# Weights copied by transfer, the last products taken tile by tile, and a new written order

## The chip, the cores and the metric

The kernel runs on one core of one Trainium2 chip. The time is device microseconds of one execution, the median of several: 563.26 us before (three runs, 563.24 to 565.26). The engines are TensorE (PE, with its weight loads as PEld), VectorE (DVE), ScalarE (ACT), GpSimd (POOL) and SyncE (SP), which issues nearly all transfers from one queue.

## The reference, cut to what matters

```python
# attention: B=4 batches, H=8 heads, S=768 steps, D=48; MoE: 3072 tokens, 384 -> 2048 -> 384
scale = np.minimum(mag, 0.999) / (mag + 1e-06)            # mag = |a_re + i a_im|
for t in range(S):
    new_re = ar * S_re - ai * S_im                        # complex decay of the state
    new_im = ar * S_im + ai * S_re
    S_re, S_im = new_re + outer(k[t], v[t]), new_im
    y[t] = q[t] @ S_re
x = y.transpose(0, 2, 1, 3).reshape(B * S, H * D)
h = x @ w_in
out = (np.maximum(h, 0) + np.log1p(np.exp(-np.abs(h)))) @ w_out
```

## The kernel before, in words

The 768 steps are cut into six groups of 128 (g = 0 to 5). In each group four chunks, one a batch, go through the recurrence in its parallel form, and the 512 tokens that they give go through the two products.

`pre` (L328) loads the decays and q and k of one or two chunks and turns them, with logarithms, exponentials, sines and running sums on ACT and DVE, into scaled q and k. `chunk` (L533) sends them by transfer into another layout (L565, L569), forms scores on PE (L633 in group 0, L637 later), masks them on DVE into the tiles `a` (L642, L645), multiplies them with v and the earlier state (L674, L677), splits the result into two float32r words in `xt` (L686, L687) and updates the state (L712, L716). From group 1 on, all of this runs PE on tiles of 32 columns or rows; everything else uses the array whole.

`moe` (L730) runs, for each of 16 blocks f of 128 hidden columns, a first product of nine matmuls of 512 columns (`mm1`, L755), a softplus (ACT L759 to L761, DVE L770 or L764), a split into `gh` and `gl` (DVE L772 or ACT L773, DVE L774), and a second product of nine matmuls (`mm2`, L790) into three banks o0, o1, o2, one for each 128 rows of the output. In group 0 the second product takes the weights as they came, in three slower float32 matmuls (L787). After it, `move` (L289) makes the two-word form of the eight w_out blocks: a copy into a free buffer `t` (L291 on ACT or L293 on DVE), a rounding (L276 or L278) and a subtraction (L279). `fin` and `closing` copy the three banks out and send them (L814 to L816, L801 and L802). Weights come as 64-bit words; `inspect` (L303) reads them again for a check, whose count (`verdict`, L890) every engine loads at the end (L915, L1149) to branch past the general program.

The planner records every operation as a task with its readers and writers. The order in which tasks are issued, and for some of them the engine (A or D behind a number), stands in the table ORDER, written out by hand; entries x and y are filler matmuls that nothing reads (L828). Buffers come from pools by tag: `t` has five, `g` six (gh, gl, two of the v tiles), `lt` two (softplus), `a` two (masked scores), `att` three banks.

Of the kernel before, what the change touches and what calls it, by code (L numbers as in the profile page):

```python
# [21 lines left out]
P = 128  # L22
# [17 lines left out]
NLT = 2  # L40
NG = 6
# [3 lines left out]
LAG = 2  # L45
NTM = 1
# [117 lines left out]
class Prog:  # L164
# [64 lines left out]
    def weights(self):  # L229
# [5 lines left out]
        for j in range(2 * NWP):  # L235
# [92 lines left out]
    def pre(self, si):  # L328
# [163 lines left out]
        def turn():  # L492
            if summed:
                for c in range(m):
                    h = slice(c * W // m, (c + 1) * W // m)
                    ab, va, _ = sums(1, c, f"o{1 + si % 2}" if first else "att", 1 if first else NATT, (part(t3, c), v3))
                    add("DVE", d1(W // m), lambda h=h, va=va: V.tensor_scalar(vn()[:, h], va(), 1.0 / TWO_PI, None, ALU.mult),
                        r=[ab], w=[part(t5, c)])
# [7 lines left out]
            add("DVE", d2(W), lambda: V.tensor_scalar(vn(), v4(), 1.0 / TWO_PI, None, ALU.mult), r=[t4], w=[t5])  # L506
# [26 lines left out]
    def chunk(self, si, c):  # L533
# [43 lines left out]
        if not last and not turned:  # L577
            for j in range(2):
# [15 lines left out]
                add("PE", 0.25, trans, r=[q for q in rs if q[1] != (zc, 1 - j)], w=[pst])  # L594
# [3 lines left out]
        if not last and turned:  # L598
            for j in range(2):
                def blocks(j=j):  # L600
                    X = half().rearrange("p (j i k t) -> p j i k t", j=2, i=NI, k=2)[:, j, :, 1]
                    o = kt().rearrange("p (q b j i) -> p j i q b", q=NQ, b=QT, j=2)[:, j]
                    V.transpose(o, X.rearrange("p i (q b) -> p i q b", q=NQ))  # L603

                add("DVE", d1(DM), blocks, r=[q for q in rs if q[1] != (zc, 1 - j)], w=[(kt, j)])
# [85 lines left out]
        if not last:  # L691
# [27 lines left out]
            add("PE", 1.5 if first else 0.75, kvmm, r=[k2 if turned else kt, vt] + ([] if first else [vo]), w=[kv], mode=0 if first else 1)  # L719
# [10 lines left out]
    def moe(self, g, dst):  # L730
# [13 lines left out]
        def mm1(f):  # L744
            h = Buf(ps, "h", [P, 512], F32, "h", 2)
            t = Buf(p, "lt", [P, GT], F32, "lt", NLT)
# [11 lines left out]
            add("PE", 9 * tmm, mm, r=[xt, w], w=[h])  # L758
# [19 lines left out]
        def mm2(f):  # L778
            gt = gs.pop(f)
            w = self.w["o", f // 2]  # L780

            def mm():
                for m in range(NI):
# [9 lines left out]
            t = add("PE", 2.57 if native("o", f) else 9 * tmm, mm, r=[*gt, w], w=acc)  # L793
# [3 lines left out]
        def closing(m):  # L797
            o = Buf(p, "t", [P, NI * 2 * CH], F32, "o", NT)

            def leave():  # L800
                A.activation(o()[:, :n], acc[m](), AF.Copy)  # L801
                nc.scalar.dma_start(dst[m * P : (m + 1) * P], o()[:, :n].rearrange("p (b t) -> p b t", b=B))  # L802
# [3 lines left out]
        def fin():  # L806
            for m in range(NI):
                if g == NGRP - 1 and m == NI - 1:
# [21 lines left out]
    def fast(self):  # L830
        with ExitStack() as ctx:
# [44 lines left out]
            cols = self.out.rearrange("d (b s) -> d b s", b=B)  # L876
            for g in range(NGRP):
                self.moe(g, cols[:, :, g * CH : (g + 1) * CH])
# [117 lines left out]
    def tokens(self):  # L996
        tc, nc = self.tc, self.nc
        V, A, G, PE = nc.vector, nc.scalar, nc.gpsimd, nc.tensor
        with ExitStack() as ctx:
# [22 lines left out]
            flat = self.toks.rearrange("b s n -> (b s) n")  # L1022
            with tc.For_i(0, NTOK, P) as t0:
                x = p.tile([P, DM], F32, tag="x", name="x")
                nc.sync.dma_start(x, flat[bass.ds(t0, P)])
# [38 lines left out]
                nc.sync.dma_start(self.out.rearrange("(m p) t -> p m t", p=P)[:, :, bass.ds(t0, P)],  # L1064
# [4 lines left out]
5 0 4 3 24 8 9 43 2 1 27 28 10 11 12 13 62 14 30 29 31 15 46 47 32D 16 33 48 17 795 49 65 821 34 18 66 50 44 805 35  # L1069
51 67 68 63 6 796 69 36 52 25 19 22 822 70D 37 823 797 53 y1 x2 38 81 87 54 798 39 82 88 83 55 20 40 801 89 84 56 21  # L1070
91 85 86 42 71 y2 x4 57 92 45 7 26 41 815 103 102 23 93 125 72 73 126 y4 x1 133 58 64 94 127 74 128 59 106 96 61 107
75 104 144 131 y3 x3 76 114 90 97 145 100 98 77 78 99 80 130 132 134 806 115 129 x3 137 101 111 138 110 95 135 142
147 150 146 148 149 136 152 108 109 105 139 143 799 112 151 163 113 824 164 140A 153 800 802 156 154 161 155 157 171
816 141 172 162 803 817 118 169 170 158 818 119 159A 819 116 117 160 166 60 165 168 167 173 807 79 175 811 182 120
121A 123 188 174 176 845 825 820 808 122 177 178A 180 179 976 189 809 804 812 977 978 979 971 190 813 191 810 980
846 871 831 208 841 192 861 972 973 974 975 826 x3 987 847 827 848 981 193 865 184 183 835 855 988 989 194 990 991
814 828 195 982 983 203 984 849 196 986 992 204 993 985 850 829D 999 197 994 995 998 205 830 198 1000 206 851 199
996 214 1001 997 207A 215 1002 200 1004 201 1005 1003 216 1010 1011 1006 124 1016 1007 1008 217 832 218 833 834 202
836 1009 837 219 229 1012 1013 230 838 231 232 839 1014 842 1015 1029 1022 255 840 1030 233 238 1031 1032 181 220
1028 1017 240 1033 221 222 223 856 843 237 234 236 185 254 235 1023 844 857 1018 1019 256 242 1020 241 239 858 224  # L1080
1021 244 257 1035 245 243 225 249 268 859 186 251 252 253 209 258 1024 1025 261 246 1026 247A 187 1036 226 250 1027
262 1034 227 272 860 269 270 278 210 279 1037 1038 266 259 260 1041 263 228 271A 1039 281 280 282 852 853 854 1047
1040 1042 1043 1044 866 867 248 283 293 868 296 1048 869 1049 1046 1052 870 1045 1050 297 862 316 213 318 1051 863
864 294 872 267 315 317 212 1059 295 300 1053 319 1060 284 285 1054 264 1055 1061 1062 286 1056 287 1058 1064 1082D
265 323 1083 299 325 873 874 320 1073 1057 321 301 298 326 1063 288 322D 324 1065 1066 1074 289 308 1075 273 1084
290 327 309 306 291 328A 1069 1067 307 1070 330 310 329 331 292 304 311A 211 1068 1071 302 312 332 333 334 1097 336
1072 305 303 313 314 1098 1099 1100 1111 335 1101 1102 1104 342 343 1112 1103 1113 1114 345 344 1105 1106 1107 1115
346 347 1076D 1108 1109 1077D 1118 1119 1127 1110 357 1116 1078 1117 1126 360 358 1120 1121 1134 1128 1122 1129 1130
361 366 385 1079 359 368 1123 1143 348 337 382 367D 386D 1124 1125 383 274 380 1080 381 275 1131 365 379 1144 384
1145 1132 349 362 363 364 276 1146 1081 350 369 1133 1147 396 1142 1135 1148A 1136 1151 1149 377 389 387 1137 1138  # L1090
1139 351 397 352 353 1152 1140A 1153 1141 398 390 354 355 356 388 1150 1159 400 277 1158 1154 406 407 1155 401 394
391 408 409 1160 1156A 1161 395 1183 1162 370 410 392A 399 393 1085 372 371 1163 1166 373 1167 374 1086D 1157 411
421 422 424 423 412 1164A 1184 1165 413 378 1185 1186 1187 1188 1189 1168 375A 429 338 376 426 427 1169 1170 428 339
# [111 lines left out]
```

## Time and profile before

| what | us |
| --- | --- |
| median of 3 runs | 563.26 |
| the profiled execution, as timed | 563.96 |
| its span, first to last instruction | 562.3 |
| PE busy | 539.1 |
| DVE busy | 440.4 |
| ACT busy | 419.8 |

The page's slices show PE at nine tenths or more from the second slice of 14 us to the last but one, at the full clock. So what counts is when PE's unbroken work starts, how much work it is, what gaps are left, and what comes after its last matmul.

### The profile page before, as it was taken

How to read it: one execution, taken by the hardware profiler on the slowest of the kernel's cores; microseconds unless marked ns; L12 is line 12 of the kernel's file. 1: busy time of each engine (PE TensorE's matmuls, PEld its weight loads, DVE VectorE, ACT ScalarE, POOL GpSimd, SP SyncE). 2: the span in 40 equal slices, each digit the busy share in tenths (PEclk: the TensorE clock that was granted, in tenths of full speed). 3: DMA queues.
4: the chain of work that ended last, by engine and by line, in shares of the span. 5: the costliest groups of instructions: out<-in, count | busy, mean ns of one | idle time of the engine just before them, and what ended most of it. 6: DMA issues, size and time to landing. Idle time of an engine off the chain costs nothing.

```text
span 562.3 us, 13185 instructions
## 1 busy us (share of the span) xinstructions
PE 539.1 (96%) x5438; PEld 420.7 (75%) x5438; DVE 440.4 (78%) x693; ACT 419.8 (75%) x716; POOL 5.7 (1%) x27
## 2 busy tenths in 40 slices
PE   1999999999999999999999999999999999999995
PEld 1688656755788788877878888788888887888883
DVE  7999999999899999989888798978895434352342
ACT  7986998686598986677858659668777647758884
POOL 4000000000000000000000000000000000000000
PEclk9999999999999999999999999999999999999998
DMA  8679914507518062285453573552644722143532
GB/s 313 261 192 365 413 54 113 163 0 186 156 39 235 30 154 89 72 237 174 122 165 110 136 203 104 135 173 65 150 125 125 203 57 85 56 128 125 161 93 59
DMA packets 49584, 81.90 MB, mean 146 GB/s; under 512 B 4336, under 2 KB 33776, under 8 KB 49520
## 3 DMA queue, kind: packets, MB, share of 16 engines
q1 hardware_dynamic: 48992, 80.76, 48.1%
q8 instruction: 43, 0.70, 0.5%
q10 hardware_dynamic: 528, 0.26, 0.2%
q14 instruction: 21, 0.17, 0.1%
HBM read 54.26 MB, written 7.86 MB: 110 GB/s over the span
## 4 chain that ended last, share of the span: by engine, by line
PE 77%; DVE 11%; ACT 7%; issue 2%; DMA 2%; SPq 0%; DVEq 0%; ACTq 0%
PE h L755 30%; PE o L790 26%; PE o L787 6%; PE att L637 4%; PE att L674 2%; PE att L677 2%; DVE t L428 2%; DVE kt L603 1%; PE att L633 1%; PE att L716 1%; PE att L584 1%; ACT L887 1%; DVE a L645 1%; DMA x<-dense_dram 1%; DMA out_dram<-o 1%
## 5 line engine op out<-in xcount | busy, mean ns | idle before, releaser
L755 PE MATMUL h<-xt,wi 128*128 128x512 f32 x864 | 217.5, 400 | 1.7 <-DVE lt L770 1.0
L755 PEld LDWEIGHTS h<-xt,wi 128*128 128x128 f32 x864 | 160.3, 188 | 44.8 <-issue 3.4
L790 PE MATMUL o<-gh,wo 128*128 128x512 f32 x480 | 160.8, 398 | 0.0
L759 ACT ACTIVATE lt<-h 128x512 f32<-128x512 f32 x96 | 56.8, 593 | 72.5 <-PE h L755 51.0
L770 DVE SCALAR_TENSOR_TENSOR lt<-h,lt 128x512 f32<-128x512 f32 x80 | 54.7, 687 | 71.1 <-ACT lt L761 70.8
L790 PEld LDWEIGHTS o<-gh,wo 128*128 128x128 f32 x480 | 90.2, 188 | 21.9 <-issue 0.6
L790 PE MATMUL o<-gl,wo 128*128 128x512 f32 x240 | 94.6, 394 | 0.3 <-DVE gl L774 0.3
L761 ACT ACTIVATE lt<-lt,fixed 128x512 f32<-128x512 f32 x96 | 68.6, 720 | 2.0
L774 DVE TENSOR_TENSOR gl<-lt,gh 128x512 fp32r<-128x512 f32 x80 | 54.3, 687 | 12.5 <-ACT gh L773 7.5
L760 ACT ACTIVATE lt<-lt 128x512 f32<-128x512 f32 x96 | 60.0, 629 | 2.0
L790 PEld LDWEIGHTS o<-gl,wo 128*128 128x128 f32 x240 | 45.2, 188 | 10.6 <-DVE gl L774 0.9
L787 PE MATMUL o<-gf,raw_wo 128*128 128x512 f32 x96 | 43.2, 594 | 0.2 <-DVE raw_wo L269 0.2
L887 ACT ACT_TABLE_LOAD x30 | 38.5, 1283 | 0.5
L428 DVE TENSOR_TENSOR_SCAN t<-hold,t 128x384 f32<-128x384 uint8 x40 | 36.1, 945 | 0.8
L645 DVE TENSOR_TENSOR a<-att,mask 128x512 f32<-128x512 f32 x40 | 26.8, 685 | 8.4 <-PE att L677 4.7
L787 PEld LDWEIGHTS o<-gf,raw_wo 128*128 128x128 f32 x96 | 17.8, 190 | 19.5 <-issue 17.2
L637 PEld LDWEIGHTS att<-qk 96*32 96x32 f32 x1280 | 25.1, 110 | 5.9 <-issue 3.3
L773 ACT ACTIVATE gh<-lt 128x512 fp32r<-128x512 f32 x28 | 17.3, 626 | 14.7 <-DVE lt L770 13.9
L637 PE MATMUL att<-qk 96*32 96x64 f32 (+3 forms) x1280 | 27.8, 235 | 0.1
L772 DVE TENSOR_SCALAR gh<-lt 128x512 fp32r<-128x512 f32 x52 | 21.8, 424 | 6.1 <-PE o L790 4.3
L477 ACT ACTIVATE x<-t 128x768 f32<-128x768 f32 x20 | 16.2, 836 | 10.1 <-DVE t L428 10.1
L524 DVE TENSOR_TENSOR x<-x,t 128x768 f32<-128x768 f32 x24 | 22.7, 951 | 0.5
(110 smaller groups left out, 681.0 us busy)
## 6 DMA issues: line engine op xcount, KB each, us to landing
x<-dense_dram SPq DMA_DIRECT2D x20, 768.0 KB, 6.1
qk<-x SPq DMA_DIRECT2D x48, 288.0 KB, 4.3
raw_wi<-w_in_dram SPq DMA_DIRECT2D x8, 768.0 KB, 9.5
raw_wo<-w_out_dram SPq DMA_DIRECT2D x8, 768.0 KB, 11.7
seen<-w_in_dram SPq DMA_DIRECT2D x16, 384.0 KB, 3.5
seen<-w_out_dram SPq DMA_DIRECT2D x16, 384.0 KB, 3.6
v<-vpad_dram SPq DMA_DIRECT2D x24, 224.0 KB, 4.4
qk<-x SPq DMA_DIRECT2D x48, 96.0 KB, 3.6
```

The source lines that it names most:

```text
L428: V.tensor_tensor_scan(out()[:, s], self.hold, inc()[:, s], 0.0, ALU.mult, ALU.add)
L637: PE.matmul(psc()[QT * u : QT * (u + 1), hh * P + f : (hh + 1) * P], q[:, h, CH + f : CH + f + QT], q[:, h, f:CH], start=True, stop=True)
L645: V.tensor_tensor(a().rearrange("p (x z) t -> p x z t", z=2), psc().rearrange("p (x z t) -> p x z t", x=2, z=2), self.mask[:, None].to_bro ...
L755: PE.matmul(h()[:, :n], w()[:, q, i, fs], xt()[:, x, i], start=k == 0, stop=k == 3 * NI - 1)
L759: add("ACT", a1(n) - 0.04, lambda: A.activation(tv(), h(), AF.Abs), r=[h], w=[t])
L760: add("ACT", a1(n), lambda: A.activation(tv(), tv(), AF.Exp, scale=-1.0), w=[t], tab="log")
L761: add("ACT", a1(n, 1), lambda: A.activation(tv(), tv(), AF.Ln, bias=self.one), w=[t], tab="log")
L770: add("DVE", d1(n), lambda: V.scalar_tensor_tensor(tv(), h(), 0.0, tv(), ALU.max, ALU.add), r=[h], w=[t])
L774: add("DVE", d1(n), lambda: V.tensor_tensor(gl(), tv(), gh().bitcast(F32), ALU.subtract), r=[t, gh], w=[gl])
L787: PE.matmul(acc[m]()[:, :n], v, gt[0](), start=f == 0, stop=f == NF - 1)
L790: PE.matmul(acc[m]()[:, :n], w()[:, wq, f % 2, ms], x(), start=f == 0 and q == 0, stop=f == NF - 1 and q == 2)
L887: nc.scalar.preload_act_table_set(TABLES[table])
```

## The change

- The copy in `move` becomes a transfer from SyncE's queue, out of the raw weights into a buffer `t`; ACT and DVE keep the rounding and the subtraction.
- In the last group the second products of the last four blocks f are twelve tasks of three matmuls, one for each f and bank, so that the written order can finish o0, then o1, then o2. Three matmuls of one f and bank are done as before.
- The output in memory is laid out by group, so that a row of one output transfer is 512 floats in one run (2 KB) instead of four runs of 128 (512 B); the host puts it back in order. The general program, which isn't run here, follows.
- `a`, `lt` and `g` share one pool of ten buffers, where they had two, two and six.
- Two more operations may be given to ACT, and some planning durations differ.
- ORDER is another sequence throughout, with 23 filler matmuls instead of 26 (ten of 512 columns in both).

```diff
-NLT = 2
-NG = 6
+NG = 10
+LAST = 4
...
-                x = add("ACT", a1(n), lambda: A.activation(bits()[:, :n].bitcast(F32), val().bitcast(F32), AF.Copy),
-                        r=[raw], w=[bits])
-                x.alt["DVE"] = (d2(n), lambda: V.tensor_copy(bits()[:, :n].bitcast(F32), val().bitcast(F32)))
+                add("SP", 0.45, lambda: nc.sync.dma_start(bits()[:, :n], val()), r=[raw], w=[bits], nbytes=4 * n * P)
...
+                    q.alt["ACT"] = (a1(W // m) - 0.05, lambda h=h, va=va: A.activation(vn()[:, h], va(), AF.Copy, scale=1.0 / TWO_PI))
...
-            a = Buf(p, "a", [P, 4, P], F32, f"a{gc}_{j}", 2)
+            a = Buf(p, "g", [P, 4, P], F32, f"a{gc}_{j}", NG)
...
-            t = Buf(p, "lt", [P, GT], F32, "lt", NLT)
+            t = Buf(p, "g", [P, GT], F32, "lt", NG)
...
-        def mm2(f):
-            gt = gs.pop(f)
+        def mm2(f, part=range(NI)):
+            gt = gs[f]
...
-                for m in range(NI):
+                for m in part:
...
-                    dst[ms], ov().rearrange("p (b t) -> p b t", b=B)), r=[o], nbytes=4 * n * P)
+                    dst[ms], ov()), r=[o], nbytes=4 * n * P)
...
+        split = NF - LAST if g == NGRP - 1 else NF
         for f in range(NF + LAG):
             if f < NF:
                 mm1(f)
-            if f >= LAG:
+            if LAG <= f < split + LAG:
                 mm2(f - LAG)
+        for m in range(NI):
+            for f in range(split, NF):
+                mm2(f, (m,))
         fin()
...
-                self.moe(g, cols[:, :, g * CH : (g + 1) * CH])
+                self.moe(g, self.out[:, g * GT : (g + 1) * GT])
...
-1764 1768
+1767 1771 1772 1774 1768 1773 1775 1776
```

Three places in the program show what the new sequence does. The first is PE's end, in the last group; o0, o1 and o2 are the output banks, gh and gl the two words of one block f. Before, the last nine matmuls are the last block's:

```order
L790 MATMUL o0_5554<-gh_5967,wo7_2329 128x512
L790 MATMUL o0_5554<-gl_5979,wo7_2329 128x512
L790 MATMUL o0_5554<-gh_5967,wo7_2329 128x512
L790 MATMUL o1_5558<-gh_5967,wo7_2329 128x512
L790 MATMUL o1_5558<-gl_5979,wo7_2329 128x512
L790 MATMUL o1_5558<-gh_5967,wo7_2329 128x512
L790 MATMUL o2_5562<-gh_5967,wo7_2329 128x512
L790 MATMUL o2_5562<-gl_5979,wo7_2329 128x512
L790 MATMUL o2_5562<-gh_5967,wo7_2329 128x512
```

After, the last twelve are all of bank o2, from four blocks f:

```order
L790 MATMUL o2_5569<-gh_5903,wo6_2248 128x512
L790 MATMUL o2_5569<-gl_5905,wo6_2248 128x512
L790 MATMUL o2_5569<-gh_5903,wo6_2248 128x512
L790 MATMUL o2_5569<-gh_5892,wo6_2248 128x512
L790 MATMUL o2_5569<-gl_5920,wo6_2248 128x512
L790 MATMUL o2_5569<-gh_5892,wo6_2248 128x512
L790 MATMUL o2_5569<-gh_5923,wo7_2334 128x512
L790 MATMUL o2_5569<-gl_5942,wo7_2334 128x512
L790 MATMUL o2_5569<-gh_5923,wo7_2334 128x512
L790 MATMUL o2_5569<-gh_5956,wo7_2334 128x512
L790 MATMUL o2_5569<-gl_5958,wo7_2334 128x512
L790 MATMUL o2_5569<-gh_5956,wo7_2334 128x512
```

So o1 is complete twelve matmuls before the end instead of three, and o0 twenty-one instead of six.

The second place is PE in group 1, between the scores of two chunks (qk7 and qk6; att0 to att2 are the banks, x_5 the turned q and k, gf the softplus of a block of group 0). Before, a transpose and six second-product matmuls stand between them:

```order
L637 MATMUL att1_92<-qk7_1239 32x128
L584 MATMUL att0_91<-ident_58,x_5_623 128x128 x3
L787 MATMUL o0_193<-gf_1346,raw_wo7_619 128x512
L787 MATMUL o1_695<-gf_1346,raw_wo7_619 128x512
L787 MATMUL o2_697<-gf_1346,raw_wo7_619 128x512
L787 MATMUL o0_193<-gf_1355,raw_wo7_619 128x512
L787 MATMUL o1_695<-gf_1355,raw_wo7_619 128x512
L787 MATMUL o2_697<-gf_1355,raw_wo7_619 128x512
L637 MATMUL att1_92<-qk6_1267 32x128
```

After, the same two chunks' scores follow each other, as do later their products with v:

```order
L637 MATMUL att0_91<-qk7_1256 32x96
L637 MATMUL att0_91<-qk7_1256 32x64
L637 MATMUL att0_91<-qk7_1256 32x32 x2
L637 MATMUL att0_91<-qk7_1256 32x64
L637 MATMUL att0_91<-qk7_1256 32x96
L637 MATMUL att0_91<-qk7_1256 32x128
L637 MATMUL att2_93<-qk6_1277 32x128
L637 MATMUL att2_93<-qk6_1277 32x96
```

PE changes between the whole array and its 32-wide tiles 74 times in the program before and 62 times in the one after.

The third place is SyncE's queue in the same stretch (vo, v: parts of v; x_6, x_7: inputs of the next chunks; o: output copies). Before:

```order
L569 DMA qk6_1267<-x_5_623 96x1x256
L565 DMA qk6_1267<-x_5_623 96x1x768
L569 DMA qk6_1267<-x_5_623 96x1x256
L565 DMA qk6_1267<-x_5_623 96x1x768
L388 DMA x_6_1082<-dense_dram 128x2x768
```

After, two of the eight weight copies (valo0, valo3) stand among these transfers:

```order
L565 DMA qk7_1256<-x_5_510 96x1x768 x2
L291 DMA valo0_1275<-raw_wo0_254 128x768
L565 DMA qk6_1277<-x_5_510 96x1x768
L569 DMA qk7_1256<-x_5_510 96x1x256
L291 DMA valo3_1301<-raw_wo3_512 128x768
L569 DMA qk6_1277<-x_5_510 96x1x256 x2
```

The queue issues in order, so what stands behind a copy also stands behind the wait for the copy's buffer.

## Rows read from the trace of the kernel before

**Rows 1.** Busy time of each engine in four stretches: us, busy (instructions), PE clock, DMA share, GB/s

```profile
0.00:33.60 33.60, 20.67 (x104) 14.79 (x104) 28.91 (x58) 29.26 (x56) 5.71 (x27) 1.00 0.77 268
33.60:58.00 24.40, 24.30 (x295) 21.89 (x295) 23.84 (x38) 16.67 (x35) 0.00 (x0) 1.00 0.92 312
58.00:546.00 488.00, 484.78 (x4999) 376.82 (x5000) 383.21 (x587) 364.82 (x607) 0.00 (x0) 1.00 0.46 132
546.00:562.30 16.30, 9.35 (x42) 7.23 (x40) 4.42 (x12) 9.00 (x21) 0.00 (x0) 0.90 0.19 51
```

**Rows 2.** Busy tenths in 40 slices of 14 us, from the page

```profile
DVE  7999999999899999989888798978895434352342
```

**Rows 3.** Waits of PE over the span: us in total, times, longest

```profile
PE sum L449 <- DVE t L419: 12.2, 1, 12.2
PE h L755 <- DVE lt L770: 1.0, 1, 1.0
```

**Rows 4.** PE from its first scores to the second pair of first products

```profile
33.59 2.05 PE L633 MATMUL att<-qk 96*128 96x128 f32 x16
...
52.78 4.46 PE L755 MATMUL h<-xt,wi 128*128 128x512 f32 x18
...
58.41 4.46 PE L755 MATMUL h<-xt,wi 128*128 128x512 f32 x18 [0.51 <-DVE gf L764]
```

**Rows 5.** Chain of waits, 545 us to the end

```profile
546.90 8.35 PE o L790 x36
...
555.33 0.60 ACT o L801
```

**Rows 6.** The last output transfer, on ACT's queue

```profile
L802 ACTq DMA_DIRECT2D out_dram<-o x1: 647/647/647, 556.0 to 556.0; - x1
...
DMA to landing us min/median/max: 4.8/4.8/4.8
```

**Rows 7.** The closing branch by engine: ns min/median/max, first and last start

```profile
L1149 SPq EVENT_SEMAPHORE  x8: 17/17/17, 557.8 to 560.9; - x8
...
L1149 ACTq EVENT_SEMAPHORE  x1: 17/17/17, 558.2 to 558.2; - x1
```

**Rows 8.** The two output transfers on SyncE's queue at the end

```profile
L816 SPq DMA_DIRECT2D out_dram<-o x2: 534/540/547, 554.5 to 555.3; - x2
...
DMA to landing us min/median/max: 2.6/2.7/2.8
```

**Rows 9.** The last block's softplus and split, in order of time

```profile
547.81 0.58 ACT L759 ACTIVATE lt<-h 128x512 f32<-128x512 f32 x1
...
551.11 0.69 DVE L774 TENSOR_TENSOR gl<-lt,gh 128x512 fp32r<-128x512 f32 x1
```

**Rows 10.** What the transfers moved, in 40 slices: 557 to 560 us, then the span

```profile
GB/s 273 300 287 314 307 294 267 287 260 280 259 273 280 287 266 294 294 280 280 396 55 130 225 14 123 0 0 0 0 0 0 0 0 0 0 7 14 7 0 0
...
GB/s 313 261 192 365 413 54 113 163 0 186 156 39 235 30 154 89 72 237 174 122 165 110 136 203 104 135 173 65 150 125 125 203 57 85 56 128 125 161 93 59
```

**Rows 11.** Chain of waits, 325 to 346 us: start, us, what

```profile
325.11 1.24 PE att L637 x34
326.36 2.31 PE o L790 x9
328.67 2.10 PE h L755 x9
...
344.88 1.11 PE att L637 x34
```

**Rows 12.** The copies of w_out by engine: busy us, mean ns, idle before

```profile
L291 ACT ACTIVATE valo<-raw_wo 128x768 f32<-128x768 f32 x5 | 4.1, 835 | 0.0
...
L293 DVE COPY valo<-raw_wo 128x768 f32<-128x768 f32 x3 | 1.7, 552 | 0.0
```

**Rows 13.** Transfers of the same size: KB each, us to landing

```profile
kd<-kt SPq DMA_DIRECT2D x8, 384.0 KB, 3.9
```

**Rows 14.** Who waited for output transfers: us, times

```profile
  ACT kt L586: 1.9, 1
```

More of the change, by code (lines that the diff above doesn't have):

```diff
@@ L505, in turn @@
             add("DVE", st, lambda: scan(1, v4, v3), r=[car[1]], w=[t3, t4] + ([] if last else [car[1]]))
-            add("DVE", d2(W), lambda: V.tensor_scalar(vn(), v4(), 1.0 / TWO_PI, None, ALU.mult), r=[t4], w=[t5])
+            q = add("DVE", d2(W) + 0.04, lambda: V.tensor_scalar(vn(), v4(), 1.0 / TWO_PI, None, ALU.mult), r=[t4], w=[t5])
+            q.alt["ACT"] = (a1(W), lambda: A.activation(vn(), v4(), AF.Copy, scale=1.0 / TWO_PI))
             add("DVE", d1(W), lambda: V.scalar_tensor_tensor(v3(), v4(), 1.0 / TWO_PI, vn(), ALU.mult, ALU.subtract),
@@ L592, in evac @@
                     copy(common[:, :, :, :, j], p3[:, :, 2 * D :].rearrange("p i (y r) -> p i y r", y=2))
-                add("PE", 0.25, trans, r=[q for q in rs if q[1] != (zc, 1 - j)], w=[pst])
+                add("PE", 0.32, trans, r=[q for q in rs if q[1] != (zc, 1 - j)], w=[pst])
                 q = add("ACT", 0.43, evac, r=[pst], w=[(kt, j)])
@@ L603, in blocks @@
                     V.transpose(o, X.rearrange("p i (q b) -> p i q b", q=NQ))
-                add("DVE", d1(DM), blocks, r=[q for q in rs if q[1] != (zc, 1 - j)], w=[(kt, j)])
+                add("DVE", 0.74, blocks, r=[q for q in rs if q[1] != (zc, 1 - j)], w=[(kt, j)])
             spill = self.dram.tile([P, NI * 2 * CH], F32, tag=f"kd{gc}", name=f"kd{gc}")
@@ L717, in kvmm @@
                                   start=h == 0, stop=h == H - 1)
-            add("PE", 1.5 if first else 0.75, kvmm, r=[k2 if turned else kt, vt] + ([] if first else [vo]), w=[kv], mode=0 if first else 1)
+            add("PE", 1.33 if first else 0.6, kvmm, r=[k2 if turned else kt, vt] + ([] if first else [vo]), w=[kv], mode=0 if first else 1)
             def reals(t):
@@ L756, in mm @@
                         k += 1
[L758 removed]
+            add("PE", 9 * tmm + 0.012, mm, r=[xt, w], w=[h])
             add("ACT", a1(n) - 0.04, lambda: A.activation(tv(), h(), AF.Abs), r=[h], w=[t])
@@ L791, in mm @@
                                   start=f == 0 and q == 0, stop=f == NF - 1 and q == 2)
-            t = add("PE", 2.57 if native("o", f) else 9 * tmm, mm, r=[*gt, w], w=acc)
+            t = add("PE", (2.57 if native("o", f) else 9 * tmm) * len(part) / NI, mm, r=[*gt, w], w=[acc[m] for m in part])
             if self.opener is None:
@@ L1020, in convert @@
                 V.tensor_tensor(lo, v, hi.bitcast(F32), ALU.subtract)
-            flat = self.toks.rearrange("b s n -> (b s) n")
-            with tc.For_i(0, NTOK, P) as t0:
+            cols = self.out.rearrange("(m p) (g b t) -> p m g b t", p=P, g=NGRP, b=B)
+            rows = self.toks.rearrange("b (g t) n -> t g b n", t=CH)
+            with tc.For_i(0, NGRP, 1) as g, tc.For_i(0, B, 1) as b:
                 x = p.tile([P, DM], F32, tag="x", name="x")
-                nc.sync.dma_start(x, flat[bass.ds(t0, P)])
+                nc.sync.dma_start(x, rows[:, bass.ds(g, 1), bass.ds(b, 1)].rearrange("t g b n -> t (g b n)"))
                 px = ps.tile([P, 512], F32, tag="px", name="px")
@@ L1203 @@
     r = run_bass_kernel_spmd(nc, [{f"{n}_dram": arr[n] for n in _INS}], core_ids=[0])
-    return np.ascontiguousarray(r.results[0]["out_0_dram"].T)
+    out = r.results[0]["out_0_dram"].reshape(DM, NGRP, B, CH)
+    return np.ascontiguousarray(out.transpose(2, 1, 3, 0)).reshape(NTOK, DM)
```

139 lines of the change are left out of this document (72 added, 67 removed), and 6 rows, old and new, of the table ORDER.

## Prediction

> **What bounds the kernel now.** I read the busy times by stretch first, then PE's waits, then the chain of waits, then the end line by line. In the long stretch from 58 to 546 us PE is busy for 484.78 of 488.00 us [rows 1]: 3.2 us are idle. DVE has 105 us to spare there and ACT 123 us, though the page's slices show DVE at nine tenths or more in 15 of slices 2 to 17, which end at 239 us [rows 2]. Before 58 us PE waits once for long, 12.2 us at the start, for the first decay sums; its longest other wait is 1.0 us [rows 3]. From 33.59 us PE works on without a gap (24.30 of 24.40 us [rows 1]) through the scores of group 0 to its first products at 52.78 us [rows 4]. After 546.90 us come 36 matmuls, 8.35 us, which end at 555.25 us [rows 5], and then 7.0 us with next to no engine at work. So a time is to be won in four places: the start of unbroken work, the work itself, 3.2 us of gaps, and the end.
>
> **The end.** The last copy out of PSUM starts at 555.33 us and takes 0.60 us [rows 5]; its transfer is issued at 556.0 us and lands 4.8 us later [rows 6], at 560.8 us. SyncE's last wait at the branch ends at 560.9 us [rows 7], and the span, of 562.3 us, ends 1.4 us on. So that landing sets the end. The two transfers ahead of it, issued at 554.5 and 555.3 us, landed after 2.6 and 2.8 us [rows 8]: the last one shared the engines with them. After the change o1 is complete twelve matmuls before the end and o0 twenty-one, at 8.35/36 = 0.232 us each 2.8 and 4.9 us before. With 0.60 us of copying and 2.8 us to land, o1's transfer lands some 0.6 us after the last matmul, when o2's is issued (0.7 us after it). So o2's goes alone. Nothing in the trace shows a lone one from ACT's queue: the bounds are 2.6 us [rows 8] and 4.8 us, unchanged [rows 6]. I take 3.0 us, near the two of the same size and time: 1.8 us gained, between 0 and 2.2. What is late next is the branch: ACT is through it at 558.2 us, 2.7 us before SyncE [rows 7], so it doesn't cut the gain off.
>
> The tile-by-tile order needs block 15 earlier. Between the last first product and block 15's first use stand 21 matmuls, 4.9 us, one more before gl is read: 5.1 us. From its first softplus step to the end of gl the block took 551.11 + 0.69 - 547.81 = 4.0 us [rows 9]. So that is covered if ACT starts it within 1.1 us; cost 0, and whatever ACT is later than that comes on top.
>
> The slices at the end, of 512 B rows, move 259 to 314 GB/s while they run; the page's fifth slice, of other transfers, 413 [rows 10]. If rows of 2 KB ran at the latter, 0.26 MB would take 0.6 us instead of 0.9, and the gain would be 0.3 us more; I count none of it. The Trainium skill, DMA: Bandwidth & Descriptors (Specifications), has 512 B as the smallest transfer that reaches line rate: by it the longer rows buy nothing, and the sum stays as it is. The same page (Anatomy of one DMA) gives a fixed cost of about 2.0 us, mostly the wait for the write to be confirmed; with 0.9 us for the bytes, an estimate by that page is 2.9 us for the last landing, a gain of 1.9 us, and no run yet shows a lone one.
>
> **The work of PE.** The matmuls are the same but for three short fillers, which lie where PE waits anyhow: nothing. But PE changes between the whole array and 32-wide tiles 62 times instead of 74, six stretches of small tiles fewer. In one place the chain shows 1.24 us for a set of scores that follows a first product and 1.11 us for one that follows other small work, and 2.31 us for the second product behind scores against 2.10 us for a product behind a product [rows 11]: 0.13 + 0.21 = 0.34 us a stretch, 2.0 us for six. These ends are modelled, and in the first three groups, where several of the six lie, DVE is nearly as full as PE and would give some of it back as waits. Between 0 and 2.0 us I take 1.2.
>
> **The gaps.** The sequence is another throughout, so each of the 3.2 us of gaps may go and others may come. The order alone doesn't tell; bounds are 3.2 us gained and a loss that the copies set (below). I take 0.
>
> **The start.** Up to the first products PE has the same work in the same kind of order, so 52.78 us stays. Two DVE instructions of 384 columns go to ACT there, and masked scores no longer wait for one of two buffers. PE's next stop is for DVE, 0.51 us before the second pair of first products at 58.41 us [rows 4]. I take 0.3 us of it, between 0 and 0.5.
>
> **The copies.** Five on ACT, 4.1 us, and three on DVE, 1.7 us, go [rows 12]; both engines have that much room, so it counts 0 by itself. In their place SyncE issues eight transfers. The nearest rows, transfers of the same 384 KB, land after 3.9 us [rows 13], against 0.835 us for a copy: the rounded weights and the buffer come 3.1 us later, eight times. Queued behind each on SyncE are the q and k of the next chunks, their v and inputs, and the outputs, and for those the scores and ACT wait. That such a wait happens shows once in before: ACT sat 1.9 us behind an output transfer that held a buffer [rows 14]; PE had other work then. I take 0, with 24.6 us of added holding (8 x 3.1) as the store that a loss can come from. The other edits, the merged pool, 2 KB rows for the earlier outputs and a few operations given to the other of ACT and DVE (an instruction for another of like length), are hidden behind PE's 99% and count 0; without that cover each is a microsecond at most.
>
> **The sum.** 1.8 + 1.2 + 0.3 = 3.3 us. The profiled execution took 563.96 us, so 560.7; it stands 0.70 us above the median of 563.26, and against that the same 3.3 us give 560.0 us.
>
> **Rivals.** (a) Only the end comes out: the six stretches and the start give nothing, since DVE sets the pace through the first groups, and small new gaps, which I put at 0.5 us, take a part of the end's gain: 563.26 - 1.8 + 0.5 = 562.0 us. For it: DVE's full slices, and that no row shows PE's gaps in the new order. Against: PE is the one without gaps, at 99%. (b) The gaps shrink too. If 2.5 of the 3.2 us go, 560.0 - 2.5 = 557.5 us. For it: the merged pool takes away waits for buffers, and 5.8 us leave ACT and DVE. Against: what is left of gaps is small waits of many kinds, of which the longest is 1.0 us. (c) Slower: the copies hold up SyncE's queue in groups 0 and 1, where two of them stand between the q and k transfers of one chunk and those of the next. If a quarter of the 24.6 us reaches PE, 6.2 us, and the end still gives its 1.8 while the rest gives nothing, the time is 563.26 + 6.2 - 1.8 = 567.7 us. It decides once the new waits pass the gains, 3.3 us; under that it only eats them. Against it: PE has other first and second products to do at most moments, and an ACT wait of 1.9 us cost it nothing. (d) The last transfer doesn't land sooner, since its 4.8 us belong to ACT's queue and not to company: then 560.0 + 1.8 = 561.8 us, in the same class as (a).
>
> **How the numbers follow.** The forecast of 560.0 us, from 558.5 to 561.5 us by itself, has 46%; (a) and (d) together 32%; (b) 12%; (c) 10%. A change of 0.5%, 2.8 us, is about what a measurement of this kernel can tell from none: under 560.4 us is faster, over 566.1 us slower. Under 560.4 us lie 0.36 of the forecast's 0.46, 0.08 of the 0.32 of (a) and (d), and all 0.12 of (b): faster 0.56. Over 566.1 us lies (c) but for its mild part: slower 0.09. The rest is no change, 0.35. The range leaves out the worst of (c) and the best of (b): 557.2 to 563.8 us.
>
> **What would show it.** The chain at the end: about 5.2 us from PE's last matmul to the end of the span instead of 7.0, with a landing near 3 us; PE's busy share from 58 us to its last matmuls still 99%, and the last matmul some 1.5 us earlier than 555.25; second-product runs behind small tiles fewer. The forecast is wrong if PE's waits in that stretch add to more than 5 us, if any of them names a weight that came by copy or a score behind SyncE's queue, or if the last landing stays at 4.8 us.

## The result and the profile after

The changed kernel takes 556.81 us (median of four runs, 556.40 to 557.65) against 563.60 us of the kernel before beside it: a ratio of 0.9876, interval 0.9852 to 0.9899. A second comparison, made later, gave 556.68 against 564.65 us, 0.9857 (0.9840 to 0.9873). So 6.8 to 8.0 us are gained where 3.3 were forecast, and the time lies below the range. The profiled execution took 556.58 us, with a span of 554.7 us.

The first view of the kernel after is the busy time of each engine by stretch, with columns as in [rows 1].

```profile
0.00:33.60 33.60, 20.22 (x101) 14.79 (x102) 28.69 (x58) 28.57 (x54) 5.68 (x27) 1.00 0.77 271
33.60:58.00 24.40, 23.66 (x293) 21.33 (x291) 23.39 (x36) 18.06 (x40) 0.00 (x0) 1.00 0.89 296
58.00:546.00 488.00, 487.08 (x5024) 382.05 (x5025) 383.62 (x597) 370.51 (x617) 0.00 (x0) 1.00 0.46 139
546.00:554.70 8.70, 3.69 (x18) 2.64 (x16) 0.21 (x2) 1.20 (x2) 0.00 (x0) 0.97 0.26 95
```

In the long stretch PE is idle for 0.9 us instead of 3.2 [rows 1], while DVE is as busy as before and ACT by 5.7 us more, in a stretch that now holds more of the work. PE's waits over the span (total, times, longest) are these:

```profile
PE sum L447 <- DVE t L417: 13.4, 1, 13.4
PE att L677 <- issue: 0.6, 1, 0.6
PE att L633 <- ACT kt L586: 0.6, 1, 0.6
PE h L755 <- DVE gf L764: 0.3, 1, 0.3
PE h L755 <- DVE lt L770: 0.2, 1, 0.2
```

The 1.0 us for a softplus on DVE [rows 3] is down to 0.2. The two waits of 0.6 us are new or longer than before, so the gaps shrank in sum and not one by one. The first wait is 1.2 us longer, and the first products start no later for it, as PE's timeline shows. It has, from the first products on:

```profile
52.70 4.45 PE L755 MATMUL h<-xt,wi 128*128 128x512 f32 x18
...
58.09 2.13 PE L755 MATMUL h<-xt,wi 128*128 128x512 f32 x8 [0.28 <-DVE gf L764]
```

The second pair starts 0.3 us earlier than in [rows 4]. The chain of waits of the kernel after, at its end:

```profile
539.14 10.44 PE o L790 x45
...
549.67 0.60 ACT o L801
```

and the last output transfer after (ns of the issue, then microseconds to landing):

```profile
L802 ACTq DMA_DIRECT2D out_dram<-o x1: 381/381/381, 550.3 to 550.3; - x1
...
DMA to landing us min/median/max: 3.0/3.0/3.0
```

The last matmul ends at 549.58 us, not 555.25 [rows 5]; from there to the end of the span it is 5.1 us, not 7.0. The transfer is issued in 381 ns, not 647, and lands after 3.0 us, not 4.8 [rows 6].

These rows split the 7.6 us by which the span is shorter: 0.3 at the start, 1.9 behind the last matmul, and 5.35 between (58.41 to 555.25 us is 496.84, 58.09 to 549.58 is 491.49), where the forecast had 1.2. Of the 5.35, 2.3 are gaps that the windows show. These rows compare one execution of each kernel; in another of the changed kernel the last matmul ended at 549.66 us. The experiments ask which part of the change did it.

### The profile page after: what moved, and what is told of

It is laid out like the page before. It is cut to its first block, busy times and chain, and to the rows that moved or that the text cites. A ratio compares the mean times of both kernels' runs of the same rounds, so it can differ in the third digit from the quotient of the medians.

```text
span 554.7 us, 13114 instructions
## 1 busy us (share of the span) xinstructions
PE 534.6 (96%) x5432; PEld 420.8 (76%) x5432; DVE 435.9 (79%) x690; ACT 418.3 (75%) x711; POOL 5.7 (1%) x27
## 4 chain that ended last, share of the span: by engine, by line
PE 88%; ACT 4%; DVE 3%; DMA 2%; issue 1%; POOL 1%; SPq 0%; DVEq 0%; ACTq 0%; POOLq 0%
PE h L755 35%; PE o L790 29%; PE o L787 7%; PE att L637 4%; PE att L674 3%; PE att L677 3%; PE att L716 2%; DMA raw_wi<-w_in_dram 1%; ACT L890 1%; PE att L584 1%; PE att L633 1%; DVE x L404 1%; PE att L712 1%; PE o L832 0%; POOL tri L216 0%
## 5 line engine op out<-in xcount | busy, mean ns | idle before, releaser
L637 PE MATMUL att<-qk 96*32 96x128 f32 (+3 forms) x1280 | 26.9, 235 | 0.0
L773 ACT ACTIVATE gh<-lt 128x512 fp32r<-128x512 f32 x33 | 20.3, 622 | 5.7 <-DVE lt L770 3.1
L677 PE MATMUL att<-a,v 128*32 128x128 f32 x640 | 22.4, 273 | 0.6 <-issue 0.6
```

What stands on the lines that cost most here:

```text
L637: PE.matmul(psc()[QT * u : QT * (u + 1), hh * P + f : (hh + 1) * P], q[:, h, CH + f : CH + f + QT], q[:, h, f:CH], start=True, stop=True)
L677: PE.matmul(o(G), v[:, w : w + 32], am[h // 4]()[:, h % 4, :], start=first and prim and G < 4, stop=not prim)
```

## The experiments

Two theories stood against each other: A, the new sequence did it, and the other edits are only what it needed; B, the other edits did it themselves, by freeing buffers and engines. Ratios are to the kernel before on the same chip, whose medians were 564.4 to 564.8 us. The changed kernel stands at 0.9857 among them, by its later comparison; by the first, 0.9876, every gain or loss against it would come out 1 us smaller. A hundredth is 5.6 us.

**One pool of ten, in the kernel before.**

```diff
-NLT = 2
-NG = 6
+NG = 10
-            a = Buf(p, "a", [P, 4, P], F32, f"a{gc}_{j}", 2)
+            a = Buf(p, "g", [P, 4, P], F32, f"a{gc}_{j}", NG)
-            t = Buf(p, "lt", [P, GT], F32, "lt", NLT)
+            t = Buf(p, "g", [P, GT], F32, "lt", NG)
```

> The kernel before, its sequence untouched, with its ten buffers for masked scores, softplus tiles and gates in one pool instead of three. Theory A (the new sequence closed the gaps and took work off PE; the other edits are only what it needed): 563.3 us, within 0.5 us of before, PE idle between 58 and 546 us near 3.2 us, since in the old sequence no PE wait names one of the three kinds of buffer. Theory B (waits for buffers were the gaps): at least 1 us less, 562.3 or under, with fewer and shorter small waits of PE.

Measured: 562.45 us, 0.9968 (0.9957 to 0.9980). Theory B, for this part. The windows row of this run for 58 to 546 us, and PE at its second pair of first products:

```profile
58.00:546.00 488.00, 485.83 (x5006) 378.13 (x5007) 383.30 (x587) 365.87 (x611) 0.00 (x0) 1.00 0.46 132
```

```profile
57.93 2.37 PE L754 MATMUL h<-xt,wi 128*128 128x512 f32 x9 [0.22 <-DVE gf L763]
```

The same sequence has 1.0 us less of gaps, and its second pair starts 0.48 us earlier. Counted from the first products (52.61 us in this run) it is 5.32 us instead of 5.63.

**Softplus tiles and gates in one pool of eight, the masked scores apart.** The edit above without its line on `a`, with NG = 8.

> The kernel before with softplus tiles and gates in one pool of eight, the masked scores apart with their two. One pool of ten gave 0.3% (1.8 us), some 0.4 us at the start of the first products and 0.8 near 120 us. Theory A (the scores' two buffers are the tight ones): within 0.5 us of before. Theory B (softplus tiles and gates are): 1.3 to 2 us less than before.

Measured: 564.57 us, 1.0006 (0.9993 to 1.0018). Theory A: softplus tiles and gates gain nothing by a common pool, so by elimination it is the two buffers of the masked scores that were tight. No run gave these alone more buffers, but the waits agree. DVE's masks wait for the products that read the scores' buffers, in the kernel before and as much in this run (us in total, times, longest):

```profile
DVE a L645 <- PE att L677: 4.7, 3, 2.6
```

```profile
DVE a L644 <- PE att L676: 5.3, 3, 2.6
```

With one pool of ten no mask waits for those products; two wait 3.3 us in all for a second product, whose gates share the pool. That the buffers held nothing up, as I had it, was wrong.

**Rows of 2 KB, in the kernel before.**

```diff
-                nc.scalar.dma_start(dst[m * P : (m + 1) * P], o()[:, :n].rearrange("p (b t) -> p b t", b=B))
+                nc.scalar.dma_start(dst[m * P : (m + 1) * P], o()[:, :n])
...
-                    dst[ms], ov().rearrange("p (b t) -> p b t", b=B)), r=[o], nbytes=4 * n * P)
+                    dst[ms], ov()), r=[o], nbytes=4 * n * P)
...
-                self.moe(g, cols[:, :, g * CH : (g + 1) * CH])
+                self.moe(g, self.out[:, g * GT : (g + 1) * GT])
```

> The kernel before with output rows of 2 KB instead of 512 B, nothing else. Theory A: it works at the end only. The last transfer is issued in 0.38 us instead of 0.65 and lands in 3.0 to 4.0 us instead of 4.8, so 1 to 2 us go: 561.3 to 562.3 us, and the last matmul stays within 0.4 us of 555.25. Theory B (the outputs' shorter landing also frees their buffers earlier, so that ACT's wait of 1.9 us for an output transfer, and PE's some 1.2 us behind it at 148 us, go): the last matmul comes 1.0 to 1.5 us earlier as well, 560.0 to 561.0 us. Theory C (the landing of 4.8 us is ACT's queue or company, not the rows): 563.0 us.

Measured: 562.47 us, 0.9962 (0.9950 to 0.9975). Its last transfer:

```profile
L802 ACTq DMA_DIRECT2D out_dram<-o x1: 381/381/381, 556.7 to 556.7; - x1
...
DMA to landing us min/median/max: 3.3/3.3/3.3
```

Theory A: the gain that the trace shows is behind the last matmul, 5.5 us instead of 7.0. The last matmul itself came no earlier: at 555.98 us it is 0.7 us later than before, more than the 0.4 us that theory A allowed, in an execution that took 0.7 us more than the median.

**Block order at the end of the changed kernel.** The last twelve second-product tasks are written f by f again.

```diff
-1758 1753 ... 1761 1754 1755 1756 1759 1760 1769D 1762 1763 1764 1770 1765 1766 1767
+1761 1753 ... 1765 1754 1755 1756 1758 1762 1766 1759 1763 1767 1760 1769D 1770 1764
```

> The changed kernel with its last four second products in block order again (each block through all four output tiles before the next), and nothing else. Rows of 2 KB alone, in the kernel before, took the stretch from the last matmul to the end of the span from 7.0 to 5.5 us, against 5.1 in the changed kernel. Theory A (the rows bring the end, the tile order only the rest): 0.3 to 0.6 us more than the changed kernel, a last landing of 3.2 to 3.4 us instead of 3.0. Theory B (as my prediction had it, that the last transfer lands sooner because it goes alone): 1.3 to 1.9 us more, a landing above 4 us.

Measured: 556.52 us, 0.9861 (0.9844 to 0.9879). The changed kernel itself wasn't among these runs, so both were run side by side later:

> The changed kernel once more, beside the version with block order at its end, so that the two are compared on one chip; the versions with one part undone ran beside the kernel before alone. All theories: 0.985 to 0.990 of before.

> The changed kernel with its last four second products in block order, once more. In the profiled executions its stretch from the last matmul to the end of the span was 4.3 us against 5.1 in the changed kernel, but its last matmul came 0.9 us later. Theory A (the tile order is worth nothing): within 0.5 us of the changed kernel. Theory B (block order is the better end, by its shorter tail): 0.5 to 1 us less. Theory C (the tile order brings part of the gain): 0.5 us or more above it.

Measured: 556.68 and 556.38 us, 0.9857 and 0.9852 (0.9834 to 0.9870). Theory A of the second expectation; of the first, theory B is refuted and theory A's loss of 0.3 to 0.6 us doesn't show. Finishing the banks tile by tile is worth nothing here that these runs can tell: in block order the last transfer landed after 2.1 us in one run and 2.9 in the other, in tile order after 3.0 and 2.7.

**Rows of 512 B in the changed kernel.** The edit on rows, taken back.

> The changed kernel with output rows of 512 B again, and nothing else. Theory A (rows work at the end only): 1.3 to 1.9 us more, issue of the last transfer near 0.65 us and landing 4 to 4.8 us, the last matmul within 0.4 us of 549.58. Theory B (rows also free buffers earlier, so some of PE's gaps belong to them): the last matmul 1 us or more later as well, 2.5 to 3.5 us more in all. Theory C (the last transfer lands sooner because it goes alone, whatever its rows): 0.2 to 0.5 us more, landing near 3.

Measured: 558.27 us, 0.9893 (0.9873 to 0.9913), 1.5 us above the changed kernel by the medians, 2.0 by the ratios. Its last transfer:

```profile
L802 ACTq DMA_DIRECT2D out_dram<-o x1: 652/652/652, 550.7 to 550.7; - x1
...
DMA to landing us min/median/max: 3.9/3.9/3.9
```

Theory A: the rows do it, and the last matmul (550.01 us) is 0.43 us later, about the 0.4 us allowed. Theory C, that the last transfer lands sooner because it goes alone, falls: it goes alone here too, since the transfer ahead of it had landed at 550.5 us. Still it landed after 3.9 us, just under theory A's 4 to 4.8; "Why the prediction was wrong" comes back to that.

**Copies by transfer, in the kernel before.** One line of the change:

```diff
-                x = add("ACT", a1(n), lambda: A.activation(bits()[:, :n].bitcast(F32), val().bitcast(F32), AF.Copy),
-                        r=[raw], w=[bits])
-                x.alt["DVE"] = (d2(n), lambda: V.tensor_copy(bits()[:, :n].bitcast(F32), val().bitcast(F32)))
+                add("SP", 0.45, lambda: nc.sync.dma_start(bits()[:, :n], val()), r=[raw], w=[bits], nbytes=4 * n * P)
```

> The kernel before with the eight copies of w_out by transfers on SyncE's queue, its sequence untouched. Theory A (the copies hold up nothing by themselves): 563.3 us, within 0.7. Theory B (5.8 us off ACT and DVE close small gaps of PE): 1 to 2 us less, 561.5 to 562.5 us. Rival (c) of the prediction (transfers stand in SyncE's queue ahead of the next inputs): 2 to 6 us more, 565 to 569 us; in a sequence that was not made for transfers this would show soonest.

Measured: 574.75 us, 1.0181 (1.0152 to 1.0210): 10.2 us slower by the ratio, more than any theory had. SyncE's own waits in this run, 195 to 216 us, then SyncE's and DVE's timelines there:

```profile
SPq L567 <- DVE x L522: 9.3, 2, 7.8
```

```profile
208.31 1.22 SPq L567 DMA_DIRECT2D qk<-x  x2
...
210.84 0.60 SPq L291 DMA_DIRECT2D valo<-raw_wo  x1
```

```profile
208.54 0.96 DVE L417 SCALAR_TENSOR_TENSOR t<-t,x 128x768 f32<-128x768 f32 x1 [0.29 <-ACT x L416]
215.80 0.56 DVE L278 CAST wo<-valo 128x768 fp32r<-128x768 f32 x1 [6.30 <-DMA valo<-raw_wo]
```

Here is rival (c) with its place. SyncE waits up to 7.8 us for rotated data before it can send pieces of q and k; the copy of block 6 stands behind these and goes out at 210.8 us. DVE is at the rounding of that block by 209.5 us and stands there until the landing at 215.8, with the scan and the softplus behind it: 1.3 us until the transfer is issued, 5.0 us more until it has landed. PE pays at its next first product:

```profile
PE h L753 <- DVE lt L768: 6.0, 2, 5.0
```

**All three edits in the old sequence.**

> The kernel before with all three: one pool, rows of 2 KB, copies by transfer; the sequence and the block order of the last second products as before. What is left between it and the changed kernel is the new sequence with the tile-by-tile end. Theory A (sequence): 561.3 to 562.5 us, that is only the end's part of the gain, and 4.5 us or more of the 6.8 are the sequence's. Theory B (the three edits bring it themselves): 558.0 to 559.5 us, and the sequence brings the remaining 1 to 3 us.

Measured: 573.69 us, 1.0167 (1.0145 to 1.0189). Neither theory had a loss. What the new sequence changes, with its end, is 17 us from here.

**Which transfers cost.** First, six of eight by transfer:

```diff
+                if b in (5, 7):
+                    add("ACT", a1(n), ...)
+                else:
                     add("SP", 0.45, ...)
```

> The kernel before with copies by transfer for six of the eight blocks; blocks 5 and 7, at whose transfers DVE stood 8.2 us between 212 and 221 us, are copied on ACT as before. Theory A (waits of the readers behind the landings): about 7 us of the 10.2 go, 566 to 568 us, and PE's wait of 5.0 us for the softplus on DVE is gone. Theory B (SyncE's queue, by the number of transfers): a quarter goes, 571 to 573 us.

Measured: 573.58 us, 1.0159 (1.0136 to 1.0182). It was aimed at the wrong blocks: I had read DVE's 8.2 us as those of 5 and 7, but 6.3 of them are block 6's, as the order of the queue shows, and they stayed. With 5, 6 and 7 on ACT:

> The kernel before with copies by transfer for blocks 0 to 4; blocks 5, 6 and 7 are copied on ACT as before. With all eight by transfer DVE stood 6.3 us for the landing of block 6, whose transfer stood on SyncE's queue behind four pieces of q and k that wait for rotated data, and 1.9 us for block 5. Theory A (the loss sits in the few readers that reach their transfer before it has landed): both waits go, and with them PE's 5.0 us wait; what is left is ACT's 2.2 to 2.9 us near 137 us: 565 to 567.5 us. Theory B (each transfer costs about 1.3 us, by contention or its place in the queue): 570 to 572 us.

Measured: 567.76 us, 1.0059 (1.0038 to 1.0080). PE's 5.0 us are gone. It is 0.3 us above theory A's range and 2.2 below theory B's; left are ACT's waits of 2.0 us on transfers near 137 us and 1.2 us that DVE waits for a copy on ACT. (Block 6 was copied on DVE before, not on ACT, so this edit moves a copy as well.) Its profiled execution, 566.0 us, was the fastest of six.

Then the transfers issued earlier and read later, with no copy given back. Only ORDER differs; on SyncE's queue, for block 6 (the names' numbers shift with it):

```diff
+L291 DMA valo_2136<-raw_wo_628 128x768
 L567 DMA qk_2143<-x_1543 96x1x256
...
 L393 DMA v_2206<-vpad_dram 128x448
-L291 DMA valo_2207<-raw_wo_628 128x768
 L563 DMA qk_2203<-x_1543 96x1x768
```

> The kernel before with copies by transfer, which took 10.2 us more than before, but with the transfers issued up to 30 places earlier in the sequence and their first readers put later, as far as the five buffers allow: 30 places between issue and reader or more for blocks 0, 2, 3, 4 and 6 (9 to 36 before), 23 for block 7 (12), 15 for block 1 (3), 8 for block 5 (5). Theory A (the loss is the reader's engine standing in line behind the landing): block 1's waits on ACT or DVE near 137 us go, some 3 us, and what block 7 waits; block 5's stays: 568 to 572 us. Theory B (the loss is SyncE's queue, in which the transfers stand ahead of the next inputs): earlier issue doesn't help, 574 us or more.

Measured: 571.44 us, 1.0120 (1.0099 to 1.0141). Theory A. The wait has moved to block 5, the one that couldn't be moved, as DVE's timeline of this run shows:

```profile
218.53 0.56 DVE L278 CAST wo<-valo 128x768 fp32r<-128x768 f32 x1 [6.19 <-DMA valo<-raw_wo]
```

And the same with that one block on ACT:

> The kernel before with transfers for seven blocks, issued earlier and read later as in the run with 571.4 us, and block 5, whose landing DVE still waited 6.2 us for there, copied on ACT. Theory A (only the landing that a reader waits for costs): DVE has no wait on a transfer, 564 to 566.5 us, no worse than 2 us above the kernel before. Theory B (each transfer costs): 569 us or more.

Measured: 564.72 us, 1.0001 (0.9990 to 1.0012). Seven transfers, no loss. The view of the copies' buffer in this run says why:

```profile
L295 SPq DMA_DIRECT2D valo<-raw_wo x7: 511/523/544, 129.0 to 209.3; - x7
...
DMA to landing us min/median/max: 2.6/3.0/5.3
```

They land after 2.6 to 5.3 us, as the eight did (2.6 to 5.2), but no reader waits for one. So in this sequence a transfer costs what its first reader stands in line for it; a price for each transfer, theory B, falls. The queue has its part in it, by when it lets the transfer go.

**Copies on ACT in the changed kernel.** The one line taken back, at the same places of the new sequence.

> The changed kernel with its eight copies of w_out back on ScalarE (8 x 0.83 us) at the same places of the sequence, and nothing else. Theory A (the transfers pay in the new sequence, since they keep 5.8 us off engines that are full there): 1 to 3 us more than the changed kernel, with PE waits that name ACT or DVE between 125 and 215 us. Theory B (the sequence is what counts and ACT has room): within 0.5 us of the changed kernel. Theory C (the transfers cost something even here): 0.5 us or more less.

Measured: 557.43 us, 0.9874 (0.9854 to 0.9894) against 0.9857 of the changed kernel: 0.75 us by the medians, 1.0 by the ratios. The intervals overlap, and by the first comparison (0.9876) nothing would be left; between theories A and B this stays open.

**Block order, copies on ACT and rows of 512 B in the changed kernel.** What stays is the sequence, with the operations that it gives to ACT, and the pool.

> The changed kernel with block order at the end, copies on ScalarE and rows of 512 B all three: what is left of the change is the new sequence and the one pool, which that sequence can't do without (it holds up to 9 gates, 4 masked scores and 4 softplus tiles, where before had 6, 2 and 2). One pool alone gained 0.3% in the old sequence (1.8 us). Theory A (sequence): the last matmul stays 3 us or more ahead of the 555.25 of before, the time 2 us above the changed kernel by the end and up to 2 more by the copies: 558.5 to 560.5 us. Theory B (the copies by transfer are what makes the sequence good): 561.5 us or more.

Measured: 558.79 us, 0.9903 (0.9884 to 0.9923). Theory A: last matmul at 550.53 us. Its windows row:

```profile
58.00:546.00 488.00, 486.27 (x5020) 381.24 (x5021) 383.11 (x591) 375.80 (x624) 0.00 (x0) 1.00 0.46 133
```

**One pool and long rows in the old sequence**, for what is left to the sequence:

> The kernel before with one pool of ten and rows of 2 KB, its own sequence, its own copies, its own end. Theory A (the parts add up): 0.9968 x 0.9962 = 0.9930 of before, 560.6 us; the changed kernel lies 2.5 to 4 us below, which is the new sequence with the copies that it was made for. Theory B (they overlap): 0.995 or more of before, and the sequence brings 4 us or more.

Measured: 561.35 us, 0.9945 (0.9929 to 0.9962). Between the theories (0.9930 and 0.995), nearer to an overlap. The changed kernel, at 0.9857, is 0.0088 below: 5.0 us are the new sequence's, with its end and the copies that it was made for. In two more pairs neither side copies by transfer. With pool and long rows the new sequence stands at 0.9874 and the old one at 0.9945, 4.0 us apart; with the pool alone they stand at 0.9903 and 0.9968, 3.7 us apart. So the order of the tasks is worth some 4 us by itself, give or take 1.5 us by the intervals, and is the largest part.

**The price of a stretch of small tiles.** Twenty short matmuls are put behind twenty products of the last group of the changed kernel, once on a 32x32 tile (first line), once on the whole array (last line).

```diff
+            self.nc.tensor.matmul(bank[:32, :64], self.ident[:32, :32], self.ident[:32, :64], start=True, stop=True)
...
+            self.nc.tensor.matmul(bank[:128, :64], self.ident[:128, :128], self.ident[:128, :64], start=True, stop=True)
```

> The changed kernel with 20 extra short matmuls of 64 columns on a 32x32 tile, one after each of 20 first and second products in the last group, where PE never waits: 20 added stretches of small tiles. Read against the next kernel, which has the same 20 matmuls on the whole array: that difference is the price of 20 changes to a small tile and back. Theory A (0.34 us a stretch, as the prediction took from the chain of waits): 6.8 us more than the next kernel. Theory B (0.15 us a stretch, as the starts of neighbouring matmuls in both traces give): 3.0 us more. Theory C (no price): the same within 0.7 us.

> The changed kernel with the same 20 extra matmuls of 64 columns at the same places, on the whole 128x128 array: 20 added matmuls and no change of tile. By the 24 ns that the tiles' rows give for 96 columns, each takes some 0.05 to 0.3 us with its weight load: 1 to 6 us more than the changed kernel in all theories; only the difference to the small tiles tells them apart.

Measured: 564.82 and 560.46 us, 1.0009 (0.9998 to 1.0020) and 0.9942 (0.9925 to 0.9958). The last chain piece of PE, on small tiles and then on the whole array:

```profile
549.82 8.58 PE o L793 x36
```

```profile
545.48 8.41 PE o L793 x36
```

The ends, 558.40 and 553.89 us, are 4.51 us apart; the medians 4.36. That is 0.22 us a stretch, between theory A (0.34) and B (0.15); it is a difference to the same short matmul on the whole array, whose own time may differ a little. The Trainium skill, TensorEngine Tiling (Array Packing) (Key Properties), says that a change of the tiling mode drains TensorE, without a price. These two runs agree that a change costs time, and give a price; the drain itself they don't show.

## Why the prediction was wrong

**The gaps: the step that failed.** The prediction has "each of the 3.2 us of gaps may go and others may come" and "I take 0". They shrank to 0.9 us, and what came is less than what went. Behind this stand two sentences that the runs contradict. One is "the merged pool, ... are hidden behind PE's 99% and count 0": by itself it gained 0.3%, 1.8 us. That PE is busy for 99% says nothing of the last hundredth, which is 5 us. The other is "an ACT wait of 1.9 us cost it nothing". I had read it from the view of waits [rows 14]; the chain of the kernel before shows it passing on to PE:

```profile
146.78 4.06 DMA out_dram<-o
...
151.26 0.60 ACT kt L586 x2
...
151.91 0.88 PE att L716 x48
```

and PE's timeline of before says what it cost:

```profile
148.60 2.73 PE L755 MATMUL h<-xt,wi 128*128 128x512 f32 x9
151.91 0.29 PE L716 MATMUL att<-v,kt 128*32 128x48 f32 x6 [0.58 <-ACT kt L586]
```

Nine matmuls, 2.10 us elsewhere [rows 11], take up 3.31 us here from start to next start. Two waits are in it. ACT's, shown as 0.58, cost 0.6 us: in the run with long rows alone PE doesn't stop at this place, and the same nine take 2.69 us:

```profile
148.13 2.73 PE L755 MATMUL h<-xt,wi 128*128 128x512 f32 x9
150.82 0.29 PE L716 MATMUL att<-v,kt 128*32 128x48 f32 x6
```

The other isn't shown as idle time at all. The second of the nine matmuls starts at 149.20 us, 0.6 us behind the first instead of 0.23, when DVE is through with the second word of `xt`:

```profile
148.59 0.56 DVE L687 TENSOR_TENSOR xt<-att,xt 128x384 fp32r<-128x384 f32 x1 [0.28 <-ACT xt L686]
```

It stands as a longer busy time, since the ends are modelled, and the kernel after has it too (146.41 and 147.00 us). So 3.2 us of idle time was less than what waits cost PE. The starts tell how much less. Matmuls of 512 columns mostly start 0.232 us apart (0.428 in float32, 0.327 ahead of small tiles). Where an interval is over 0.06 us longer, the excess adds up, from the second pair of first products on, to 10.0 us at 58 places before and 6.9 us at 47 places after: 3.1 us less, against the 0 that I took. In the kernel after, ACT no longer waits for an output transfer; who waits for one there is this alone (PEld is PE's weight load):

```profile
  PEld att L637: 0.4, 1
```

**The work of PE: right in size, in part by luck.** I took 1.2 us for six stretches less, between 0 and 2.0 by 0.34 each. Five of the six lie behind the second pair of first products, by the traces, and at 0.22 they make 1.1 us. The price was a third lower than I had it, and I had cut the 2.0 to 1.2 for another reason, waits for DVE. Of the 5.35 us between start and last matmul this leaves 4.2 for waits: the 3.1 above, of which 2.3 are seen as gaps, and 1.1 as a remainder that nothing here traces to a place.

**The end: right size, wrong cause.** 1.8 us forecast, 1.9 found, with the landing at 3.0 us as assumed. But I gave it to the tile order, by which the last transfer goes alone, and counted nothing for the rows. The runs turn that round: rows of 2 KB alone took the tail from 7.0 to 5.5 us, and block order gave the tile order's time. Not all of it is the rows. With rows of 512 B in the new sequence the last transfer landed after 3.9 us and the tail was 6.1 us, in tile order and in block order alike, where the old sequence had landings of 4.8 to 5.2 us. So about 1 us of the 1.9 came with the new sequence, neither by the rows nor by going alone, and its cause stays open; that the sum fitted was luck. The Trainium skill, DMA: Bandwidth & Descriptors (Specifications), was weighed there, with 512 B as the smallest transfer at line rate, so that longer rows buy nothing. Here the measurement decides against that use of it: in the kernel before they bought 1.5 us by the tail and 1.9 by the medians, partly in the issue itself, 381 ns for 647.

**The start: right**, 0.3 us, and it is the masked scores' buffers: from the first products to the second pair it is 5.32 us with one pool, and 5.63 with the scores apart (52.53 to 58.17 us) as before (52.78 to 58.41).

**The copies: 0 was right for this sequence only.** The prediction named the store, 24.6 us (8 x 3.1 is 24.8), and the queue, and put 10% on rival (c). In the old sequence it came as described, and cost more. In the new one no engine stands for a copy, as SyncE's and ACT's timelines of the kernel after show for the two closest pairs near 210 us:

```profile
205.74 0.52 SPq L291 DMA_DIRECT2D valo<-raw_wo  x1
...
208.14 0.51 SPq L291 DMA_DIRECT2D valo<-raw_wo  x1
```

```profile
210.26 0.83 ACT L276 ACTIVATE wo<-valo 128x768 fp32r<-128x768 f32 x1
...
213.65 0.84 ACT L276 ACTIVATE wo<-valo 128x768 fp32r<-128x768 f32 x1
```

4.5 and 5.5 us lie between issue and reader, and no wait stands in front of either reading; the eight landings took 2.6 to 4.7 us. That could have been looked for ahead of the result: the order of instructions shows the reader's distance from the issue.

**The rivals.** What came is (b), "the gaps shrink too", with both of its reasons: the pool, shown, and the copies off ACT, worth up to 1 us, not settled. The largest part, the order of the tasks, isn't among its reasons. (b) was given 557.5 us and 12%; it stayed 0.7 us above the time, and it counted only gaps that are seen. (a) and (d) are out: gaps went, and the landing shortened.

## What to carry to other kernels

Where the bounding engine is at 99%, the last hundredth can still be a prize (here waits on PE shrank by 3 to 4 us): follow each wait of a helper engine down the chain to that engine before calling it free, and compare starts with starts, because a wait can be booked as work. Buffers' counts and rows' lengths are cheap edits to try alone, also in the sequence that is there. A copy handed to a transfer cost nothing here where it had landed when its first reader came, and up to 5 us of the bounding engine where it hadn't; so look at how far the reader is from the issue, and at what stands ahead of the transfer on the queue.

## What the runs showed of the hardware

- A short matmul on a 32x32 tile between products on the whole array cost 0.22 us more than the same matmul on the whole array, in and out together (4.4 us over twenty).
- Issuing an output transfer of 256 KB took 380 to 382 ns with rows of 2 KB and 642 to 656 ns with rows of 512 B on ACT's queue; the last one landed after 2.1 to 3.3 us in nine runs with long rows (in a tenth, whose issue took 1733 ns, after 4.1) and with short ones after 4.8 to 5.2 us in the old sequence and 3.9 us in the new.
- A transfer of 384 KB inside SBUF landed after 2.6 to 5.2 us in the run with all eight copies by transfer in the old sequence, 3.7 in the middle.
